# First-layer stream in threes of cycles, f16 parts of H on GpSimd, and both halves of V in one stationary operand, in a fused attention and feed-forward kernel

## The chip, the cores and the metric

One core of one Trainium2 chip runs the kernel. The metric is the device time in microseconds, the median of several runs. Engines are named as in the profile: PE (TensorE), ACT (ScalarE), DVE (VectorE), POOL (GpSimd), SP (SyncE).

## The reference

All inputs are float32; x is [1, 2048, 512], with 32 heads of 16 that share one K and one V, and a hidden layer of 1792.

```python
x = A_x
g = _sigmoid((x * gate_w).sum(-1, keepdims=True))
# attention, H = 32, Dh = 16
q = (x @ wq).reshape(B, S, H, Dh).transpose(0, 2, 1, 3)
k, v = x @ wk, x @ wv
p = softmax(einsum("bhqd,bkd->bhqk", q, k) * Dh ** -0.5)
a = einsum("bhqk,bkd->bhqd", p, v).transpose(0, 2, 1, 3).reshape(B, S, H * Dh) @ wo
# feed-forward
b = silu(x @ w1) @ w2
return g * a + (1 - g) * b
```

## The kernel before

float32 products are made from 16-bit parts: a number is split into an f16 part and an f16 remainder, and three products of parts stand for one product. A prologue (`first_pass`) transposes x, makes K and V and the first Q. Then `attention` runs one long stream.

The stream goes through 32 rounds: 4 blocks of 512 queries, 4 groups of 8 heads, and two halves of 4 heads each (`rb`). A round has 16 steps; a step is one tile of 128 keys. Two steps make a cycle, so there are 256 cycles, and one more that only drains. The order of PE's work in a cycle is written out by hand as a string of slots, each of eight matmuls on 64x32 tiles of the array with 512 columns:

- S: scores of one pair of heads-times-queries (`scores`), and behind it one exponential on ACT, 128x1024, into the tile P (float32). A cycle has four.
- F: eight matmuls of the other work (`stream`): Q blocks, the feed-forward's first layer (`ffn_h`, into H) and second layer (`ffn_o`), and the output projection (`out_proj`). An output (`Out`) has 12 products (6 in a group with two hidden tiles); the first half of the rows of a new output runs beside the second half of the one before.
- P: one third of the product of probabilities and V in 16-bit parts (`pv` with n = 0, 1, 2): the upper halves of P by VH, the same by VL, and the remainders L by VH. L is made on DVE by `low`, two instructions of 128x1024 for a step.
- N: the same product of a step straight in float32 (`pv` with n = 3, by VF).
- B: the bound of a Q block, where there is one.

The odd step of a cycle always goes through N. The even one goes through L and three P (SPLIT), or through N (NATIVE), as `split_step` decides when its L is to be made: not in a round's first step, and not when an output of the first layer is about to end. `debt` counts F slots that the Q blocks took beyond six a cycle; when it is 6 or more and a first-layer output has just ended, the next cycle is WIDE, with 12 F.

`spend` adds up DVE's work of a cycle in an account, `put` defers small DVE work by some cycles, and `fill` does deferred work, splitting of weights (`split_pieces`) and range checks (`chores`) while the account has room; what is over goes into `backlog`.

At the end of a first-layer output ACT makes e = tanh, DVE makes e = (e + 1) * ph, and later the two parts of H:

```python
H = Hs[k, f] = wp.tile([128, 2, 512], F16, name="H", bufs=2 * NF)
spend(0.62)
put(1.0, 2, lambda: split_v(H[:, 0], H[:, 1], e))
```

At the end of a round `norm_a` on DVE transposes the two PSUM banks of the product with V into T and U, adds them and divides by the row sums in column 16 (V carries a column of ones); `norm_b` and `norm_c` transpose back and split into f16 parts. The banks have one buffer. After the last cycle the remaining outputs run plainly (`whole`).

POOL has the start's memsets and issues the loads of raw weight tiles, each when DVE has used the tile before.

Of the kernel before, what the change touches and what calls it, by code (L numbers as in the profile page):

```python
# [6 lines left out]
F32 = mybir.dt.float32  # L7
# [16 lines left out]

SPLIT, NATIVE = "SFFFSFFFSPPPSBN", "SFFFSFFFSNBSN"
WIDE = {SPLIT: "SFFFFFFSFFFFFFSPPPBSN", NATIVE: "SFFFFFFSFFFFFFSNBSN"}
# [11 lines left out]
          (26, 27, 1.0, 6e4), (27, 28, 1.0, 6e4), (28, 29, 1.0, 6e4), (29, 30, 1.0, 6e4),  # L40
# [5 lines left out]
def kernel(  # L46
# [21 lines left out]
    nc = tc.nc  # L68
# [16 lines left out]
    VH = consts.tile([128, NKT, 32], F16)  # L85
    VL = consts.tile([128, NKT, 32], F16)
    VF = consts.tile([128, NKT, 32], F32)
    gg = consts.tile([128, NKT], F32)
# [119 lines left out]
    for t_ in (VH, VL, VF):  # L208
        nc.gpsimd.memset(t_, 0.0)
    nc.gpsimd.memset(VH[:, :, 16:17], 1.0)  # L210
    nc.gpsimd.memset(VF[:, :, 16:17], 1.0)
# [139 lines left out]
    def first_pass():  # L351
        with ExitStack() as pro:
# [132 lines left out]
            v_parts()  # L485
# [15 lines left out]
    def second_pass():  # L501
        with ExitStack() as pro:
# [81 lines left out]
            scales(sb, ps, ev, vm, (2.0 ** 13,))  # L584
            nc.vector.tensor_scalar(VF[:, :, 0:16], pv_[:, :, 0:16], ev[:, 0:1], None, op0=OP.mult)
            v_parts()
# [114 lines left out]
    def attention(ctx, scale_of, t_scale, shifts, split_pieces, chores, q_todo, bounds, early, gates_):  # L701
# [79 lines left out]
        def ffn_h(k, f):  # L781
            c, g = blocks[k]
            f0 = (sum(GF[:g]) + f) * 128
            cs = slice(c * 512, c * 512 + 512)

            def evict(ph):

                e = wp.tile([128, 512], F32, name="e", bufs=2)
                nc.scalar.activation(e, ph, AF.Tanh, scale=t_scale)  # L789
                nc.vector.scalar_tensor_tensor(e, e, 1.0, ph, op0=OP.add, op1=OP.mult)  # L790
# [69 lines left out]
        def outs():  # L860

            for k in range(len(blocks) + 1):
                if k < len(blocks):
                    for f in range(GF[blocks[k][1]]):
                        yield ffn_h(k, f)
                        while urgent:
                            yield urgent.pop(0)()
                else:
                    for _ in range(2):
                        yield urgent.pop(0)() if urgent else None  # L870
                if k:
                    for t in range(4):
                        if queue:
                            debt[0] += 12
                            yield q_block(queue.pop(0))
                        yield ffn_o(k - 1, t)
                        while urgent:
                            yield urgent.pop(0)()
            while True:
                yield urgent.pop(0)() if urgent else None  # L880
# [9 lines left out]
        seq, ahead, ended, debt = outs(), [], [None], [18]  # L890
        drains = [0]
# [4 lines left out]
        def stream():  # L896

            cur = None
            while True:
                if plain[0] and cur is None:  # L900
                    o = follow()
                    if o is None:
                        return
# [25 lines left out]
                cur = new  # L929
# [9 lines left out]
        def norm_a(pv, rb, st):  # L939
# [5 lines left out]
            nc.vector.tensor_tensor(T3[:, :, 0:17], T3[:, :, 0:17], U3[:, :, 0:17], op=OP.add)  # L945
# [80 lines left out]
        def pv(s, n):  # L1026
# [5 lines left out]
            if n == 3:  # L1032
                a, b = VF[:, k], probs.pop(s)
            else:
                while n == 2 and lq and lq[0][1] == s:
# [3 lines left out]
                if n == 2:  # L1039
                    probs.pop(s)  # L1040
# [22 lines left out]
        qtile, wide = {}, [False]  # L1063
# [3 lines left out]
        for s in range(0, len(steps) + 2, 2):  # L1067
# [7 lines left out]
            p, more = 2 * s, True  # L1075
            slots, order = SPLIT, [(s - 2, 0), (s - 2, 1), (s - 2, 2), (s - 1, 3)]
# [4 lines left out]
            wide[0] = debt[0] >= 6 and ended[0] is not None and ended[0].hidden  # L1081
            if wide[0]:
                slots = WIDE[slots]
            ended[0], n_f, bounded[0] = None, 0, False
            for a in slots:
# [5 lines left out]
                elif a == "F" and more:  # L1091
                    more = not next(work)
# [12 lines left out]
            fill(4.95 if n_f > 6 else 4.1 if ended[0] and ended[0].hidden else 3.7)  # L1105
# [39 lines left out]
```

## Time and profile before

| | |
|---|---|
| median of 3 runs | 1079.02 us (1078.17 to 1079.59) |
| span of the profiled execution | 1075.3 us; its own run time is not given |
| granted PE clock, mean | 0.998 |
| first exponential starts, last ends | 39.26 us, about 1054.2 us |
| PE, ACT, DVE, POOL busy | 1057.2, 1008.6, 789.9, 23.4 us |
| exponentials, tanh | 1024 and 56 |
| L instructions on DVE | 348, two for each of 174 split steps |

A row of a group reads: line, engine, operation, output<-inputs, shapes, count | busy us, mean ns of one | idle time of the engine ahead of it, and who ended it. A row of a timeline reads: start us, duration us, engine, line, operation, output<-inputs, count, and in brackets the idle time before. Successive matmuls overlap, so that the distance of two starts, not a duration, tells what a slot takes.

### The profile page before, as it was taken

What the parts mean: (1) busy time and instruction counts of PE and PEld (TensorE: products, weight loads), DVE (VectorE), ACT (ScalarE), POOL (GpSimd) and SP (SyncE); (2) the same over time, 40 slices, a digit from 0 to 9 for tenths busy, and PEclk for the clock granted to TensorE, in tenths of its full rate; (3) what the DMA queues carried; (4) which work ended last, traced back from release to release, by engine and by line L of the source; (5) the groups of instructions that cost most, each with busy time, mean ns of one, the idle gap of its engine ahead of it and who ended that gap; (6) DMA issues with size and microseconds to landing.
All of it is one profiled execution on the core that took longest, in us unless ns stands there. A gap on an engine that the chain in (4) does not pass through costs nothing.

```text
span 1075.3 us, 65967 instructions
## 1 busy us (share of the span) xinstructions
PE 1057.2 (98%) x31224; PEld 667.5 (62%) x31224; DVE 789.9 (73%) x1082; ACT 1008.6 (94%) x1121; POOL 23.4 (2%) x53
## 2 busy tenths in 40 slices
PE   8999999999999999999999999999999999999996
PEld 5455776766665577677655568677756555555552
DVE  6856986968778786878777697675857767476875
ACT  5799999999999999999999999899989999999992
POOL 2110000000000000000000000000000000000000
PEclk9999999999999999999999999999999999999999
DMA  5311111220001000000000100000000110000001
GB/s 208 115 61 45 49 42 31 61 60 14 11 11 41 32 22 10 17 12 12 22 11 21 37 19 21 22 12 11 20 6 12 31 31 12 11 11 5 11 4 43
DMA packets 20840, 32.95 MB, mean 31 GB/s; under 512 B 5137, under 2 KB 12050, under 8 KB 20562
## 3 DMA queue, kind: packets, MB, share of 16 engines
q1 hardware_dynamic: 17618, 20.46, 5.9%
q0 software_dynamic: 2512, 8.13, 2.6%
q8 instruction: 246, 4.03, 1.5%
q14 instruction: 32, 0.26, 0.1%
q10 hardware_dynamic: 432, 0.07, 0.0%
HBM read 20.12 MB, written 8.52 MB: 27 GB/s over the span
## 4 chain that ended last, share of the span: by engine, by line
PE 89%; DVE 5%; ACT 4%; issue 1%; POOL 0%; POOLq 0%; ACTq 0%
PE pv L1043 35%; PE pm L741 31%; PE S L997 19%; ACT P L1000 4%; DVE L L1021 1%; PE pm L745 1%; PE pt L311 0%; PE pk L126 0%; DVE xs L117 0%; DVE T L943 0%; PE pk L127 0%; PE pk L125 0%; DVE U L944 0%; PE pm L342 0%; DVE T L945 0%
## 5 line engine op out<-in xcount | busy, mean ns | idle before, releaser
L1000 ACT ACTIVATE P<-S 128x1024 f32<-128x1024 f32 x1024 | 963.5, 1051 | 24.6 <-PE S L997 19.4
L997 PE MATMUL S<-qb,KT 50*32 50x512 f16 x8192 | 480.1, 378 | 2.3 <-ACT P L1000 2.2
L1021 DVE TENSOR_TENSOR L<-P 128x1024 f16<-128x1024 f32 x348 | 408.1, 1217 | 8.3 <-ACT P L1000 8.2
L1043 PE MATMUL pv<-P,VF 64*32 64x512 f32 x5408 | 374.8, 589 | 0.0
L997 PEld LDWEIGHTS <-KT 50*32 50x32 f16 x8192 | 188.6, 90 | 193.9 <-issue 126.7
L741 PE MATMUL pm<-w2s,H 64*32 64x512 f16 x5232 | 258.8, 375 | 0.6 <-DVE qx L825 0.2
L741 PE MATMUL pm<-xs,w1s 64*32 64x512 f16 x5376 | 248.5, 375 | 1.1 <-issue 0.6
L741 PEld LDWEIGHTS <-H 64*32 64x32 f16 x5232 | 143.7, 93 | 43.5 <-issue 11.3
L741 PEld LDWEIGHTS <-w1s 64*32 64x32 f16 x5376 | 136.3, 93 | 46.1 <-issue 13.5
L1043 PEld LDWEIGHTS pv<-P,VF 64*32 64x32 f32 x5408 | 125.0, 107 | 30.3 <-issue 8.1
L790 DVE SCALAR_TENSOR_TENSOR e<-e,pm 128x512 f32<-128x512 f32 x56 | 38.5, 687 | 140.3 <-ACT e L789 139.4
L1043 PE MATMUL pv<-P,VH 64*32 64x512 bf16 x1392 | 81.9, 389 | 0.0
L1043 PE MATMUL pv<-L,VH 64*32 64x512 f16 x1392 | 81.4, 374 | 0.0
L1043 PE MATMUL pv<-P,VL 64*32 64x512 bf16 x1392 | 81.4, 385 | 0.0
L741 PE MATMUL pm<-xs,wqs 64*32 64x512 f16 x1152 | 81.1, 375 | 0.0
L1043 PEld LDWEIGHTS <-VH 64*32 64x32 f16 x2784 | 60.7, 92 | 20.4 <-issue 3.8
L741 PE MATMUL pm<-wo_s,O 64*32 64x512 f16 x1440 | 63.3, 375 | 0.0
L943 DVE STREAM_TRANSPOSE T<-pv 128x512 f32<-128x512 f32 x32 | 23.0, 717 | 48.0 <-PE pv L1043 40.4
L722 DVE SCALAR_TENSOR_TENSOR acc<-pm,g,acc 128x512 f32<-128x512 f32 x48 | 35.8, 745 | 26.4 <-PE pm L741 24.6
L741 PEld LDWEIGHTS <-wqs 64*32 64x32 f16 x1152 | 43.6, 93 | 10.1 <-issue 2.8
L121 DVE TENSOR_TENSOR H<-e,H 128x512 f16<-128x512 f32 x56 | 38.8, 693 | 1.9
L789 ACT ACTIVATE e<-pm 128x512 f32<-128x512 f32 x56 | 34.5, 616 | 5.7 <-PE pm L741 5.7
(155 smaller groups left out, 478.9 us busy)
## 6 DMA issues: line engine op xcount, KB each, us to landing
qb<-qd SPq DMA_DIRECT2D x192, 32.0 KB
raw<-in_B_w_dram POOLq DMA_DIRECT2D x23, 256.0 KB, 2.9
xn<-in_A_x_dram SPq DMA_DIRECT2D x8, 512.0 KB
out_dram<-acc SPq DMA_DIRECT2D x16, 256.0 KB
qd<-qx SPq DMA_DIRECT2D x12, 256.0 KB
raw<-in_A_wo_dram POOLq DMA_DIRECT2D x4, 256.0 KB, 3.6
qb<-sh SPq DMA_DIRECT2D x62, 2.0 KB
raw<-in_B_w_dram SPq DMA_DIRECT2D x3, 256.0 KB
```

The lines of the kernel that those rows point to most:

```text
L121: nc.vector.tensor_tensor(a2, a, a1, op=OP.subtract)
L722: nc.vector.scalar_tensor_tensor(a, po, gate[:, n:n + 1], a, op0=OP.mult, op1=OP.add)
L741: nc.tensor.matmul(self.bank[32 * m:32 * m + 32], l(i, rows, 32 * m), r(j, rows), start=first, stop=last)
L745: nc.tensor.matmul(self.bank, l(i, slice(0, 128), 0, 128), r(j, slice(0, 128)), start=first, stop=last)
L789: nc.scalar.activation(e, ph, AF.Tanh, scale=t_scale)
L790: nc.vector.scalar_tensor_tensor(e, e, 1.0, ph, op0=OP.add, op1=OP.mult)
L943: nc.vector.transpose(T, pv[0])
L997: nc.tensor.matmul(sc[32 * m:32 * m + 32, f], KT[b:b + 50, k0:k0 + 32], qtile[i][b:b + 50, j], start=True, stop=True)
L1000: nc.scalar.activation(P[:, 2 * j:2 * j + 2], sc, AF.Exp, scale=scale_of(c, o))
L1021: nc.vector.tensor_tensor(lows[s][:, q], P[:, q], upper(P)[:, q], op=OP.subtract)
L1043: nc.tensor.matmul(pvs[i][h][32 * j:32 * j + 32], a[r], b[r, j], start=first, stop=last)
```

## The change

Seven things change together.

1. V's halves go into one stationary operand VP of 32 columns: 16 upper columns, the ones, and 15 lower columns. The lower part of the column 0 is written as six digits into the rounding of the columns 1 to 6, which `v_parts` computes with some 25 more small DVE operations, and `norm_a` puts together again: it adds all 32 columns of T and U, multiplies six columns by the digits' weights, adds lower to upper columns, and sums the digits. A split step has two P slots in place of three.
2. `split_step` asks only for DVE's account: the step is split if `backlog` is below 1.0 (and it isn't the round's first).
3. WIDE is gone. When `debt` is 6 or more and a first-layer output with an even number has just begun, three cycles follow with 8 F slots each, the middle one with its P and N in another order.
4. The two parts of H are made on POOL, straight behind DVE's e.
5. Outputs of the output projection come in only after every second first-layer output.
6. The stream no longer ends early: the drain's F slots are kept, and `debt` starts at 0 where there are no Q blocks to come.
7. The range in which the maximum of V is accepted is narrower (512 to 8000), with another target scale in `second_pass`, which only runs when a range check fails.

In the built program 215 even steps are split and 41 are native. The cycles of the stream become 146 SPLIT, 28 NATIVE and 81 in threes (68 with two P, 13 native), besides the first and the drain.

```diff
-SPLIT, NATIVE = "SFFFSFFFSPPPSBN", "SFFFSFFFSNBSN"
-WIDE = {SPLIT: "SFFFFFFSFFFFFFSPPPBSN", NATIVE: "SFFFFFFSFFFFFFSNBSN"}
+SPLIT, NATIVE = "SFFFSFFFSPPSBN", "SFFFSFFFSNBSN"
+PAIR = ({SPLIT: "SFFFFSFFFFSPPSBN", NATIVE: "SFFFFSFFFFSNBSN"},
+        {SPLIT: "SFFFFSPPSNSFFFF", NATIVE: "SFFFFSNSNSFFFF"},
+        {SPLIT: "SFFFFSFFFFSPPSBN", NATIVE: "SFFFFSFFFFSNBSN"})
...
-    def v_parts():
-        nc.vector.tensor_copy(VH[:, :, 0:16], VF[:, :, 0:16])
-        nc.vector.tensor_tensor(VL[:, :, 0:16], VF[:, :, 0:16], VH[:, :, 0:16], op=OP.subtract)
+    def v_parts(pool):
+        n = 1 + DIGITS
+        R, r, J = (pool.tile([128, NKT, n], F32, name=f"v{q}") for q in "RrJ")
+        y = pool.tile([128, NKT, 1], F32, name="vy")
...
+        for d in range(1, n):
+            j = J[:, :, d:d + 1]
+            nc.vector.tensor_scalar(j, y, BASE, MAGIC, op0=OP.mult, op1=OP.add)
+            nc.vector.tensor_scalar(j, j, MAGIC, None, op0=OP.subtract)
+            if d < n - 1:
+                nc.vector.scalar_tensor_tensor(y, y, BASE, j, op0=OP.mult, op1=OP.subtract)
+        nc.vector.scalar_tensor_tensor(VP[:, :, 0:n], J, GRID, R, op0=OP.mult, op1=OP.add)
+        nc.vector.scalar_tensor_tensor(VP[:, :, 17:16 + n], J[:, :, 1:n], -GRID, r[:, :, 1:n], op0=OP.mult, op1=OP.add)
...
-                spend(0.62)
-                put(1.0, 2, lambda: split_v(H[:, 0], H[:, 1], e))
+                spend(0.69)
+                nc.gpsimd.tensor_copy(H[:, 0], e)
+                nc.gpsimd.tensor_tensor(H[:, 1], e, H[:, 0], op=OP.subtract)
...
-                         lambda j, b, kt=kt: xs[b, j, kt, cs]) for kt in range(KD)], evict, hidden=True)
+                         lambda j, b, kt=kt: xs[b, j, kt, cs]) for kt in range(KD)], evict, hidden=1 + f % 2)
...
-            nc.vector.tensor_tensor(T3[:, :, 0:17], T3[:, :, 0:17], U3[:, :, 0:17], op=OP.add)
+            nc.vector.tensor_tensor(T, T, U, op=OP.add)
+            z = U3[:, :, 0:DIGITS]
+            nc.vector.tensor_tensor(z, T3[:, :, 17:17 + DIGITS], mu[:, :, 1:].to_broadcast([128, 16, DIGITS]), op=OP.mult)
+            nc.vector.tensor_tensor(T3[:, :, 1:16], T3[:, :, 1:16], T3[:, :, 17:32], op=OP.add)
+            nc.vector.tensor_reduce(U3[:, :, 16:17], z, axis=AX.X, op=OP.add)
+            nc.vector.tensor_tensor(T3[:, :, 0:1], T3[:, :, 0:1], U3[:, :, 16:17], op=OP.add)
...
-            return steps[s][1] > 0 and not (turn[0] and turn[0].hidden and (0 < turn[1] <= 6 or wide[0]))
+            return steps[s][1] > 0 and backlog[0] < 1.0
...
-                a = (VH, VL, VH)[n][:, k]
-                b = lows.pop(s) if n == 2 else upper(probs[s])
+                a = VP[:, k]
+                b = lows.pop(s) if n else upper(probs[s])
...
-                spend(2.4)
+                spend(3.1)
...
-            wide[0] = debt[0] >= 6 and ended[0] is not None and ended[0].hidden
-            if wide[0]:
-                slots = WIDE[slots]
+            if not pair[0] and debt[0] >= 6 and s and turn[0] and turn[0].hidden == 1 and turn[1] == 12:
+                pair[0] = 3
+            if pair[0]:
+                slots = PAIR[3 - pair[0]][slots]
...
-            fill(4.95 if n_f > 6 else 4.1 if ended[0] and ended[0].hidden else 3.7)
+            fill(4.1 if pair[0] or ended[0] and ended[0].hidden else 3.7)
+            pair[0] = max(pair[0] - 1, 0)
```

More of the change, by code (lines that the diff above doesn't have):

```diff
@@ L865, in outs @@
                         yield ffn_h(k, f)
[L866 removed]
+                        while urgent and f % 2:
                             yield urgent.pop(0)()
@@ L888, in follow @@
             return o
-        seq, ahead, ended, debt = outs(), [], [None], [18]
-        drains = [0]
+        seq, ahead, ended, debt = outs(), [], [None], [18 if q_todo else 0]
+        drains, over = [0], [False]
         turn = [None, 0]
@@ L928, in stream @@
                     ended[0] = cur
-                cur = new
+                cur = turn[0] = new
+                turn[1] = 12
                 if cur:
@@ L1061, in early_products @@
                 yield
-        qtile, wide = {}, [False]
+        qtile, pair = {}, [0]
         whole_ = early_products()
@@ L1074, in attention @@
                     queue.append(q_todo.pop(0))
-            p, more = 2 * s, True
-            slots, order = SPLIT, [(s - 2, 0), (s - 2, 1), (s - 2, 2), (s - 1, 3)]
+            p = 2 * s
+            slots, order = SPLIT, [(s - 2, 0), (s - 2, 1), (s - 1, 3)]
             if s - 2 in native:
@@ L1090, in attention @@
                     next(whole_, None)
-                elif a == "F" and more:
-                    more = not next(work)
+                elif a == "F":
+                    next(work)
                     n_f += 1
```

41 lines of the change are left out of this document (28 added, 13 removed).

## The prediction

> **What bounds the kernel now.** I read the page first: busy shares, the chain that ended last, the costliest groups.
>
> ```profile
> span 1075.3 us, 65967 instructions
> PE 1057.2 (98%) x31224; PEld 667.5 (62%) x31224; DVE 789.9 (73%) x1082; ACT 1008.6 (94%) x1121; POOL 23.4 (2%) x53
> PE 89%; DVE 5%; ACT 4%; issue 1%; POOL 0%; POOLq 0%; ACTq 0%
> L1000 ACT ACTIVATE P<-S 128x1024 f32<-128x1024 f32 x1024 | 963.5, 1051 | 24.6 <-PE S L997 19.4
> L1021 DVE TENSOR_TENSOR L<-P 128x1024 f16<-128x1024 f32 x348 | 408.1, 1217 | 8.3 <-ACT P L1000 8.2
> ```
>
> PE carries the chain, but ACT is only a few per cent behind it. So the question is how much less PE work helps before ACT holds the end. The stream from the first exponential to the last, in the view by windows (busy PE, PEld, DVE, ACT, POOL), is
>
> ```profile
> 39.26:1054.20 1014.94, 1011.02 (x30944) 643.19 (x30946) 754.60 (x1001) 985.77 (x1080) 16.50 (x30) 1.00 0.08 24
> ```
>
> Two timelines give the prices inside it: first one whole SPLIT cycle on PE (lines of the F slots left out), then ACT.
>
> ```profile
> 598.20 0.41 PE L997 MATMUL S<-qb,KT 50*32 50x512 f16 x8
> 599.07 0.41 PE L997 MATMUL S<-qb,KT 50*32 50x512 f16 x8
> 599.94 0.41 PE L997 MATMUL S<-qb,KT 50*32 50x512 f16 x8
> 600.16 0.42 PE L1043 MATMUL pv<-P,VH 64*32 64x512 bf16 x8
> 600.38 0.42 PE L1043 MATMUL pv<-P,VL 64*32 64x512 bf16 x8
> 600.61 0.41 PE L1043 MATMUL pv<-L,VH 64*32 64x512 f16 x8
> 600.83 0.41 PE L997 MATMUL S<-qb,KT 50*32 50x512 f16 x8
> 601.04 1.05 PE L1043 MATMUL pv<-P,VF 64*32 64x512 f32 x16
> 601.90 0.41 PE L997 MATMUL S<-qb,KT 50*32 50x512 f16 x8
> ```
>
> ```profile
> 941.69 1.94 ACT L1000 ACTIVATE P<-S 128x1024 f32<-128x1024 f32 x2
> 943.51 0.60 ACT L789 ACTIVATE e<-pm 128x512 f32<-128x512 f32 x1
> 943.99 13.88 ACT L1000 ACTIVATE P<-S 128x1024 f32<-128x1024 f32 x15
> ```
>
> Not the durations count here (they overlap) but the starts. A slot of eight matmuls takes 0.22 us, whether S, F or P; the f32 slot N takes 0.86, that is four slots. The cycle has 4 S, 6 F, 3 P and one N: 17 slots in 601.90 - 598.20 = 3.70 us, **0.218 a slot**. ACT, when nothing holds it, starts an exponential every (943.51 - 941.69)/2 = **0.91 us** and loses **0.48** to a tanh. A cycle of four exponentials is 3.64, with a tanh 4.12.
>
> Before, by the order that the program is built in: 162 SPLIT cycles of 17 slots (3.70), 66 NATIVE of 18 (3.92; 35 of them with a tanh, 4.12), 11 and 16 wide ones of 23 and 24 slots (5.01, 5.23), and a first one of 5.0 (in both sums): 599.4 + 121.5 + 144.2 + 138.8 + 5.0 = 1008.9 us. The row says 1014.9, so 6 us are stalls. The wide cycles are PE's by far, 5.01 and 5.23 against ACT's 4.12.
>
> **The change, part by part.**
>
> *V joined and the split by account.* A split step costs PE two slots in place of three. In the built order 215 even steps are split (174 before) and 41 native. Together with the threes, the cycles become 146 SPLIT of 16 slots, 28 NATIVE of 18, and 81 in threes: 68 of 18 slots and 13 of 20. PE's share is then 16 x 0.218 = 3.49, below ACT's 3.64, in the 146: ACT sets them. The 28 stay at 3.92. A three with its two tanhs is ACT's too, 3 x 3.64 + 2 x 0.48 = 11.88 against PE's 54 x 0.218 = 11.77; a cycle of 20 slots adds 0.40.
> Sum: 146 x 3.64 + 28 x 3.92 + 27 x 11.88 + 13 x 0.40 + 5.0 + 1 (two tanhs elsewhere) = 531.4 + 109.8 + 320.8 + 5.2 + 6.0 = 973.2. **Less 35.7 us.** PE alone goes from 4583 to 4328 slots, 56 us less; the other 20 stay with ACT, whose floor lets a SPLIT cycle gain only 0.06, so nearly all of the gain is that of the wide and native cycles.
>
> *DVE's load.* It pays 82 more L at 1.14 (half of 2.27, the start-to-start pace of a pair) = 93 us, and a longer norm_a. It loses the H parts. Rows of both:
>
> ```profile
> L121 DVE TENSOR_TENSOR H<-e,H 128x512 f16<-128x512 f32 x56 | 38.8, 693 | 1.9
> L120 DVE CAST H<-e 128x512 f16<-128x512 f32 x56 | 23.7, 423 | 0.6
> L790 DVE SCALAR_TENSOR_TENSOR e<-e,pm 128x512 f32<-128x512 f32 x56 | 38.5, 687 | 140.3 <-ACT e L789 139.4
> L945 DVE TENSOR_TENSOR T<-T,U 128x272 f32<-128x272 f32 x32 | 14.2, 444 | 1.1
> L950 DVE TENSOR_TENSOR C<-T,rr 128x256 f32<-128x256 f32 x32 | 13.6, 425 | 1.1
> L947 DVE RECIPROCAL rr<-T 128x16 f32<-128x16 f32 x32 | 8.1, 254 | 1.1
> ```
>
> The parts go: 38.8 + 23.7 = 62.5 us. norm_a's addition grows from 0.44 to about 0.69 (the 128x512 row), and four operations are new: one of 240 elements (0.42), a product and a reduction of 96 (0.25 to 0.42 each), one of 16 (0.15 to 0.25): 1.4 us more a round. DVE comes to 754.6 + 93 - 62.5 + 31 x 1.4 = 829 us of about 979, 85% against 74%. It does not become the bound by sum; its lateness counts where PE needs an L.
>
> *At a round's end.* There norm_a stands ahead of the next L on DVE:
>
> ```profile
> 590.89 0.72 DVE L943 STREAM_TRANSPOSE T<-pv 128x512 f32<-128x512 f32 x1 [2.70 <-PE pv L1043]
> 593.35 0.74 DVE L722 SCALAR_TENSOR_TENSOR acc<-pm,gg,acc 128x512 f32<-128x512 f32 x1
> 594.01 4.62 DVE L1021 TENSOR_TENSOR L<-P 128x1024 f16<-128x1024 f32 x4
> ...
> 596.90 0.41 PE L1043 MATMUL pv<-L,VH 64*32 64x512 f16 x8
> ```
>
> The first pair of L is done at 594.01 + 2.27 = 596.28, and PE asks for it at 596.90. With 1.4 more it is done at 597.68; PE asks one slot earlier, about 596.67, and waits 1.0. Behind that P stands the next S, and behind it ACT. But where ACT is the bound PE is 0.91 - 0.22 = 0.69 ahead of it, so 0.3 is lost: 31 x 0.3 = **9 us**. Ends: 0 where no operation of another part stands between, 31 x 1.4 = 43 with no lead at all.
>
> *H parts on POOL.* Before, POOL does almost nothing:
>
> ```profile
> L178 POOL DMA_DIRECT2D raw<-in_B_w_dram x27 | 14.7, 544 | 186.0 <-DVE w1s L196 99.8 <-DVE w2s L196 64.0 <-DVE wqs L196 14.2
> L304 POOL COPY wkv<-wvr 128x64 f32<-128x64 f32 x1 | 0.2, 237 | 0.0
> L305 POOL COPY wkv<-gwr 128x4 f32<-128x4 f32 x1 | 0.2, 190 | 1.0 <-DMA gwr<-in_gate_w_dram 1.0
> ```
>
> The two copies differ by 47 ns for 60 elements, so a copy of 512 is some 0.19 + 0.40 = 0.59 us; the subtraction, with two operands, from the same to 0.19 + 2 x 0.40 = 0.99. That is 1.2 to 1.6 us for an H, 56 x 1.6 = 90 us of an idle engine. H is read a block later, so nobody waits for it, and the tile e has two buffers against an H every 1.5 cycles. Behind each part on POOL stand the raw weight loads (27 of w1 and w2 by the row, six others): a load now waits up to a tanh and two parts more, some 4 us, and its raw tile is asked for three cycles (11 us) later. I cost that at nothing; with that cover gone it would be 4 us for each of the loads that come late, which ends with the last weight.
> Whether POOL slows DVE no row of before shows, for POOL computes nothing while DVE does. Ends: a gain of 0 (DVE isn't the bound) and all of POOL's time taken from DVE. A three gives DVE 6 L (6.8), two e (1.4) and 3/8 of a norm_a of 3.9 (1.4), 9.6 of 11.88: 2.2 us are free, 1.1 for each H. As 1.2 to 1.6 is near that, I take 0.1 for each of 54: **5 us**.
> [...]
>
> *The start.* v_parts grows by 25 operations: 18 on 128x16 (0.17 each by the row below), seven on 112 elements a partition (0.2 to 0.25): 3.1 + 1.6 = 4.7 us more on DVE.
>
> ```profile
> L329 DVE TENSOR_SCALAR gg<-gg 128x16 f32<-128x16 f32 x1 | 0.2, 169 | 0.0
> ```
>
> ```profile
> 39.76 0.69 DVE L824 TENSOR_SCALAR O<-pm 128x512 f16<-128x512 f32 x1 [1.72 <-PE pm L745]
> 40.49 0.69 DVE L825 SCALAR_TENSOR_TENSOR O<-pm,O 128x512 f16<-128x512 f32 x1
> 42.50 0.39 PE L342 MATMUL pm<-qx,kab 64*32 64x512 f16 x2
> ```
>
> DVE has 1.72 idle ahead of the first eviction, and the matmul that takes over the evicted bank comes 42.50 - 41.18 = 1.3 after it. 4.7 - 1.7 - 1.3 = 1.7, rounded to **2 us**. Ends: 0 and 4.7.
>
> *The end.* The last norm_a is on the path (1.4), and 24 plain products stand there for 18:
>
> ```profile
> 1060.41 4.47 PE L745 MATMUL pm<-wo_s,O 128*128 128x512 f16 x12 [2.21 <-DVE O L120]
> 1064.90 4.04 PE L745 MATMUL pm<-w2s,H 128*128 128x512 f16 x18
> ```
>
> 6 x 4.04/18 = 1.3, together **3 us**.
>
> Sum: 1075.3 - 35.7 + 9 + 5 + 2 + 3 = 1058.6, the 6 us of stalls left in. No time of the profiled execution itself is given; the median of the runs, 1079.02, lies 3.7 above its span. **Forecast 1062 us.**
>
> **The rivals.**
>
> *ACT runs free.* The lead of 0.69 hides norm_a and POOL, and most of the old 6 us too: 1062 - 9 - 5 - 5 = 1043. For it: what ACT waited for ahead of an exponential was PE, 19.4 of 24.6 us, and PE now has slots to spare. Against: the L of the round's end above stood only 0.62 ahead of PE, before DVE's load grew.
>
> *DVE late at more places.* At every round's end 0.7 instead of 0.3, by the same row with an eviction more: 12 us more, 1074.
>
> *POOL holds DVE (slower than before).* Beside an L each part takes DVE's turn. If all 1.6 of an H are lost to DVE, 0.5 beyond the free 1.1, it costs 54 x 0.5 = 27 instead of 5: 1084. The point from which it decides: slower than 1081 from 0.45 beyond the free time, 1.55 us an H. For it: L follows e directly on DVE, just when POOL begins. Against: a part that comes first delays one L, and DVE is idle behind many an e (the 139.4 us of its row).
> [...]
>
> *The change doesn't do what it says.* That fewer steps are split than meant, or that cycles stay wide, the built order excludes.
>
> **How the numbers follow.** Forecast 0.56 (its own range 1050 to 1070); ACT free 0.18 (1040 to 1050); DVE late 0.15 (1070 to 1080, a fifth of it within 0.2% of before, about what a measurement here can tell from no change); POOL holds DVE 0.11. Faster 0.86, same 0.03, slower 0.11. 1041 to 1078 leaves out about 0.16.
>
> **What would show it.** Right: P slots go in pairs, SPLIT cycles at 3.6 to 3.7 with exponentials at 0.91 without idle, threes near 11.9, ACT's busy share at 96% or more, PE's idle rows before P named after DVE's L and only behind norm_a. Wrong: threes over 12.3 with L lasting longer than 1.22 or starting late beside POOL (the last rival), or a SPLIT cycle below 3.6 (then ACT's floor is lower than 0.91). If the first exponential starts 4 us later, v_parts was mis-costed.

## The result, and the profile after

The changed kernel is slower: 1094.35 us (median of 4 runs, 1092.31 to 1097.11) against 1079.3 us for the kernel before in the same session (4 runs, 1078.17 to 1080.89). The ratio is 1.0144, with a 95% interval of 1.0125 to 1.0163. The forecast was 1062 us and its range ended at 1078, so direction and size were both wrong.

The page of the kernel after, in the rows that answer to those of before: span, busy shares, the chain that ended last, the exponentials, L.

```profile
span 1095.2 us, 63374 instructions
PE 1050.2 (96%) x29790; PEld 577.0 (53%) x29790; DVE 899.7 (82%) x1206; ACT 1012.1 (92%) x1121; POOL 215.0 (20%) x170
PE 66%; DVE 26%; ACT 5%; issue 2%; DMA 0%; another core or an unknown queue 0%; ACTq 0%; POOL 0%; DVEq 0%
L1035 ACT ACTIVATE P<-S 128x1024 f32<-128x1024 f32 x1024 | 968.4, 1067 | 44.0 <-PE S L1032 32.8
L1056 DVE TENSOR_TENSOR L<-P 128x1024 f16<-128x1024 f32 x430 | 531.0, 1281 | 11.1 <-ACT P L1035 11.1
```

And the stream, from the first exponential to the last, in the view by windows (busy PE, PEld, DVE, ACT, POOL):

```profile
39.38:1071.20 1031.82, 1001.38 (x29468) 551.41 (x29474) 860.76 (x1109) 989.03 (x1080) 208.82 (x142) 1.00 0.09 24
```

What to see: in the chain DVE went from 5% to 26%, and PE from 89% to 66%. The exponentials wait longer for PE's scores (32.8 us, 19.4 before), although PE issues 1434 fewer matmuls. In the stream DVE was to be busy 829 us of 979; it is busy 861 of 1032, 83%. PE is busy 97% of it, ACT 96% and DVE 83%, and in the chain they take turns: they wait for each other. The window ends 0.2 us before the last exponential, at 1071.38; with that the stream grew by 17.1 us (1014.9 to 1032.0) and what comes behind it by 2.7.

The cycles by kind, from the start of every fourth exponential in the trace (sums over the kind, us):

| kind | count | forecast | after | after, DVE's extra work gone (after_all_short) |
|---|---|---|---|---|
| SPLIT | 146 | 531.4 | 551.0 (median 3.64, mean 3.77) | 539.8 |
| NATIVE | 28 | 109.8 | 121.4 | 113.5 |
| in threes | 81 | 326.0 | 351.8 | 344.5, a pause of about 5 in it |
| first | 1 | 5.0 | 7.6 | 5.0 |

Half of the SPLIT cycles do run at the forecast pace; the mean is what the forecast missed. The last column is a run of experiment 9 below, which leaves work out. Three places in the trace show why.

**A round's end.** Timelines of DVE, PE and ACT in the kernel after, around the end of a round that falls into the middle of a three (some DVE lines left out):

```profile
504.20 0.72 DVE L973 STREAM_TRANSPOSE T<-pv 128x512 f32<-128x512 f32 x1 [2.85 <-PE pv L1078]
...
507.89 0.71 DVE L989 STREAM_TRANSPOSE T<-C 128x512 f32<-128x512 f32 x1
508.53 0.65 DVE L815 SCALAR_TENSOR_TENSOR e<-e,pm 128x512 f32<-128x512 f32 x1
509.10 2.76 DVE L1056 TENSOR_TENSOR L<-P 128x1024 f16<-128x1024 f32 x2
511.78 1.39 DVE L124 CAST O<-T 128x512 f16<-128x512 f32 x1
```

```profile
507.53 0.42 PE L1032 MATMUL S<-qb,KT 50*32 50x512 f16 x7
509.23 0.37 PE L766 MATMUL pm<-xs,wqs 64*32 64x512 f16 x1 [1.28 <-DVE e L815]
```

```profile
505.43 0.62 ACT L814 ACTIVATE e<-pm 128x512 f32<-128x512 f32 x1
505.90 3.11 ACT L1035 ACTIVATE P<-S 128x1024 f32<-128x1024 f32 x3
510.63 2.05 ACT L1035 ACTIVATE P<-S 128x1024 f32<-128x1024 f32 x2 [1.62 <-PE S L1032]
```

The tanh is done at 506.05, but e, which empties its PSUM bank, starts only at 508.53: in DVE's queue it stands behind the whole of norm_a (504.20 to 507.85) and norm_b's transpose, which follows at once (to 508.60). PE's next F slot needs that bank, waits, and the score behind it and the exponential behind that wait too, 1.62 us on ACT. It isn't the L that is late, as I had it, but the eviction. That cycle takes 6.1 us; five of the six native middle cycles do.

**The start.** PE's timeline, DVE's, and the window of the first two cycles:

```profile
42.39 0.41 PE L1032 MATMUL S<-qb,KT 50*32 50x512 f16 x8
44.86 0.39 PE L367 MATMUL pm<-qx,kab 64*32 64x512 f16 x2 [2.06 <-DVE O L851]
```

```profile
35.95 0.23 DVE L343 CAST VP<-VF 128x144 f16<-128x144 f32 x1
...
42.05 0.25 DVE L359 SCALAR_TENSOR_TENSOR VP<-vJ,vr 128x96 f16<-128x96 f32 x1
...
44.11 0.69 DVE L851 SCALAR_TENSOR_TENSOR O<-pm,O 128x512 f16<-128x512 f32 x1
```

```profile
39.40:58.00 18.60, 16.54 (x248) 7.30 (x254) 14.95 (x38) 12.04 (x13) 2.51 (x4) 0.82 0.38 112
```

v_parts holds DVE from 35.95 to 42.30. The first exponential isn't later (39.38 against 39.26), but the eviction behind v_parts is, PE stands 2.06 us, and then the granted clock halves: 0.82 in the window, which is half speed for 6.8 of 18.6 us. The first two cycles take 7.58 and 6.95 us, 5.01 and 3.95 in the kernel before.

**DVE's and POOL's new groups.** Rows of the groups, kernel after:

```profile
L818 POOL CAST H<-e 128x512 f16<-128x512 f32 x56 | 85.2, 1521 | 641.3 <-DVE e L815 639.9 <-issue 1.5
L819 POOL TENSOR_TENSOR H<-e,H 128x512 f16<-128x512 f32 x56 | 106.5, 1902 | 4.5
L975 DVE TENSOR_TENSOR T<-T,U 128x512 f32<-128x512 f32 x32 | 22.4, 700 | 1.1
L977 DVE TENSOR_TENSOR U<-T,mu 128x96 f32<-128x96 f32 x32 | 8.3, 259 | 1.1
L978 DVE TENSOR_TENSOR T<-T 128x240 f32<-128x240 f32 x32 | 12.8, 401 | 0.0
L979 DVE TENSOR_REDUCE U<-U 128x16 f32<-128x96 f32 x32 | 7.9, 246 | 0.0
L980 DVE TENSOR_TENSOR T<-T,U 128x16 f32<-128x16 f32 x32 | 6.1, 191 | 1.1
```

norm_a grew by (0.700 - 0.444) + 0.259 + 0.401 + 0.246 + 0.191 = 1.35 us a round: sized right, placed wrong. An H costs POOL 3.42 us where I had 1.2 to 1.6, and an L 1281 ns in place of 1217.

### The profile page after: what moved, and what is told of

It is laid out like the page before. It is cut to its first block, busy times and chain, and to the rows that moved or that the text cites. A ratio compares the mean times of both kernels' runs of the same rounds, so it can differ in the third digit from the quotient of the medians.

```text
span 1095.2 us, 63374 instructions
## 1 busy us (share of the span) xinstructions
PE 1050.2 (96%) x29790; PEld 577.0 (53%) x29790; DVE 899.7 (82%) x1206; ACT 1012.1 (92%) x1121; POOL 215.0 (20%) x170
## 4 chain that ended last, share of the span: by engine, by line
PE 66%; DVE 26%; ACT 5%; issue 2%; DMA 0%; another core or an unknown queue 0%; ACTq 0%; POOL 0%; DVEq 0%
PE pv L1078 23%; PE pm L766 23%; PE S L1032 16%; DVE L L1056 10%; ACT P L1035 4%; DVE T L975 1%; DVE T L973 1%; DVE U L974 1%; DVE e L815 1%; ACT e L814 1%; PE pm L770 1%; DVE O L124 1%; DVE mxs L139 1%; DVE C L985 1%; DVE acc L747 1%
## 5 line engine op out<-in xcount | busy, mean ns | idle before, releaser
L1035 ACT ACTIVATE P<-S 128x1024 f32<-128x1024 f32 x1024 | 968.4, 1067 | 44.0 <-PE S L1032 32.8
L1056 DVE TENSOR_TENSOR L<-P 128x1024 f16<-128x1024 f32 x430 | 531.0, 1281 | 11.1 <-ACT P L1035 11.1
L1078 PE MATMUL pv<-P,VF 64*32 64x512 f32 x4752 | 333.1, 593 | 0.0
L818 POOL CAST H<-e 128x512 f16<-128x512 f32 x56 | 85.2, 1521 | 641.3 <-DVE e L815 639.9
L766 PEld LDWEIGHTS <-w1s 64*32 64x32 f16 x5376 | 119.2, 93 | 64.3 <-issue 20.9
L766 PEld LDWEIGHTS <-H 64*32 64x32 f16 x5184 | 120.4, 93 | 60.4 <-issue 18.8
L1078 PEld LDWEIGHTS pv<-P,VF 64*32 64x32 f32 x4752 | 103.0, 107 | 29.4 <-issue 4.0
L1078 PE MATMUL pv<-L,VP 64*32 64x512 f16 x1720 | 113.6, 375 | 4.5 <-DVE L L1056 3.4
L819 POOL TENSOR_TENSOR H<-e,H 128x512 f16<-128x512 f32 x56 | 106.5, 1902 | 4.5
L1078 PEld LDWEIGHTS <-VP 64*32 64x32 f16 x3440 | 71.0, 93 | 54.0 <-issue 29.4
L1078 PE MATMUL pv<-P,VP 64*32 64x512 bf16 x1720 | 99.4, 388 | 0.0
```

Source lines behind the costliest of these rows:

```text
L766: nc.tensor.matmul(self.bank[32 * m:32 * m + 32], l(i, rows, 32 * m), r(j, rows), start=first, stop=last)
L818: nc.gpsimd.tensor_copy(H[:, 0], e)
L819: nc.gpsimd.tensor_tensor(H[:, 1], e, H[:, 0], op=OP.subtract)
L1035: nc.scalar.activation(P[:, 2 * j:2 * j + 2], sc, AF.Exp, scale=scale_of(c, o))
L1056: nc.vector.tensor_tensor(lows[s][:, q], P[:, q], upper(P)[:, q], op=OP.subtract)
L1078: nc.tensor.matmul(pvs[i][h][32 * j:32 * j + 32], a[r], b[r, j], start=first, stop=last)
```

## The experiments

Ratios are to the kernel before, run beside each (its medians all lay near 1079 us); the kernel after stands at 1.0144. Differences between kernels are taken between ratios, 0.001 being 1.08 us.

**1. H parts back on DVE, where POOL made them.** Is it POOL that slows DVE down?

```diff
-                nc.gpsimd.tensor_copy(H[:, 0], e)
-                nc.gpsimd.tensor_tensor(H[:, 1], e, H[:, 0], op=OP.subtract)
+                split_v(H[:, 0], H[:, 1], e)
```

> The changed kernel with the two parts of H on DVE, at the same place and with the same account, so that the order of PE's work stays. If POOL's parts hold DVE's two-operand instructions (3.4 us of POOL for each H in the changed kernel's trace), this is faster than 1094 by 10 to 25 us, though DVE has 1.1 us more of its own for each H, and L falls back from 1281 to about 1217 ns. If the longer norm_a ahead of the evictions is what costs, it is no faster than 1094, rather 5 to 15 us slower, as DVE has 62 us more to do.

1111.38 us, ratio 1.0297 [1.028, 1.0314]: 16.5 us slower than after, a little more than the 5 to 15 expected if norm_a is what costs. Its L and its PE wait, from the groups and the waits (us, times, longest); the like wait in after is 3.4 us:

```profile
L1055 DVE TENSOR_TENSOR L<-P 128x1024 f16<-128x1024 f32 x430 | 503.0, 1217 | 8.6 <-ACT P L1034 8.6
```

```profile
PE pv L1077 <- DVE L L1055: 18.1, 32, 1.0
```

L alone is 1217 again, so POOL does lengthen it; but 1.1 us of parts ahead of L cost far more than that. In this kernel the move to POOL helps, so the rival on the slower side does not explain the loss; what POOL's reads cost by themselves experiment 5 shows.

**2. The kernel before with the H parts on POOL.**

```diff
-                put(1.0, 2, lambda: split_v(H[:, 0], H[:, 1], e))
+                put(1.0, 2, lambda: None)
+                nc.gpsimd.tensor_copy(H[:, 0], e)
+                nc.gpsimd.tensor_tensor(H[:, 1], e, H[:, 0], op=OP.subtract)
```

> The kernel before with the parts of H on POOL and nothing else changed. If POOL holds DVE, L and CAST grow where they meet a part, and the time is 1079 to 1090 although DVE loses 62 us of work. If POOL costs DVE nothing, it is 1076 to 1079, since in the old kernel PE is the bound.

1079.67 us, ratio 1.0006 [0.9996, 1.0016]: no change. L is lengthened here nearly as much, and nothing comes of it where DVE has room and gives up 62 us of parts:

```profile
L1023 DVE TENSOR_TENSOR L<-P 128x1024 f16<-128x1024 f32 x348 | 427.2, 1273 | 10.5 <-ACT P L1002 10.4
```

**3. norm_a without the digits' four operations** (the lower columns are left out).

```diff
-            nc.vector.tensor_tensor(T, T, U, op=OP.add)
...
-            nc.vector.tensor_tensor(T3[:, :, 0:1], T3[:, :, 0:1], U3[:, :, 16:17], op=OP.add)
+            nc.vector.tensor_tensor(T3[:, :, 0:17], T3[:, :, 0:17], U3[:, :, 0:17], op=OP.add)
```

> The changed kernel with norm_a as short as before (the lower columns and the digits are left out of the sum, so only upper halves come out). If the longer norm_a ahead of evictions and L is what costs, the cycles of 6 us at the round's ends fall below 5 and the time goes to 1065 to 1080. If POOL's parts are the cost, it stays within 5 us of 1094.

1076.35 us, ratio 0.9973 [0.9963, 0.9982]: 18.5 us of the kernel after go with 32 x 1.35 = 43 us of DVE work. The 6.1 us cycles become 4.99, the native ones of 5.98 become 4.86, SPLIT's sum falls from 551.0 to 543.2. The first F slot behind such a norm_a on PE:

```profile
498.87 0.37 PE L766 MATMUL pm<-xs,wqs 64*32 64x512 f16 x1 [0.16 <-DVE e L815]
```

0.16 us in place of 1.28. PE's waits for e, by the waits view of after and of this run:

```profile
PE pm L766 <- DVE e L815: 7.1, 6, 1.3
PE pm L766 <- DVE e L815: 0.8, 5, 0.2
```

With the waits for the other evictions (qx, acc) PE stands 20.2 us of the stream, from 58 us on, in after and 6.3 here; these 14 us less of waiting are most of the 18.5. Eight of the SPLIT cycles that fall, from 4.25 to 3.63, are a round's second cycle and wait for such an eviction too. Of the costs taken out one by one this is the largest.

**4. V's parts by two operations** (the lower part of column 0 is left out).

```diff
-        n = 1 + DIGITS
...
+        nc.vector.tensor_copy(VP[:, :, 0:16], VF[:, :, 0:16])
+        nc.vector.tensor_tensor(VP[:, :, 17:32], VF[:, :, 1:16], VP[:, :, 1:16], op=OP.subtract)
```

> The changed kernel with V's parts made by two operations (no digits; the lower part of V's column 0 is left out). If the start costs what the trace shows (the first two cycles 14.5 us against 8.8, part of it at half of PE's clock), the time is 1094 - 5.7 = 1088 to 1089. If the half clock has another cause than PE's wait for DVE, only some 2 us go: 1092.

1090.09 us, ratio 1.0103 [1.0086, 1.012]: 4.4 us. The first cycle is 5.01 again and no half clock follows it: the next 13 exponentials run in 12.87 us without idle. Up to 5.7 were expected with the half clock and 2 without it; how much of a run is at half clock differs between runs of one kernel (last section).

**5. POOL writes constants into H and reads nothing.**

```diff
-                nc.gpsimd.tensor_copy(H[:, 0], e)
-                nc.gpsimd.tensor_tensor(H[:, 1], e, H[:, 0], op=OP.subtract)
+                nc.gpsimd.memset(H[:, 0], 0.01)
+                nc.gpsimd.memset(H[:, 1], 0.0)
```

> The changed kernel with POOL writing constants into both parts of H instead of computing them (the parts are left out, POOL reads nothing); all else and the order of work as in the changed kernel. If the two engines meet where both read, L falls from 1281 to about 1217 ns and CAST O from 723 to 421, 430 x 64 ns = 28 us of DVE go, and the time falls from 1094 by 5 to 15 us. If the lengthened L do not reach the end, it stays within 3 us of 1094.

1091.24 us, ratio 1.0117 [1.01, 1.0134]: 2.9 us, less than the 5 to 15 expected. L is back at its old length, 1217 ns on average over all 430, though POOL still writes both parts of H (0.53 us each), so what lengthens L comes with the parts that read. (The casts of O on DVE are not back at 421 ns but at 544, from 723.) L's row:

```profile
L1056 DVE TENSOR_TENSOR L<-P 128x1024 f16<-128x1024 f32 x430 | 503.0, 1217 | 9.0 <-ACT P L1035 9.0
```

**6 and 7. The same work later.** First norm_a's transposes at once and the rest at the end of the next cycle; then v_parts too, moved behind the first cycle's work.

```diff
+            def rest():
...
+            due.append((cycle[0] + 1, rest))
...
-                spend(3.1)
+                spend(1.4)
...
+            while due and due[0][0] <= cycle[0]:
+                due.pop(0)[1]()
             fill(4.1 if pair[0] or ended[0] and ended[0].hidden else 3.7)
```

> The changed kernel with norm_a cut in two: the two transposes at once, which free the banks, and the rest at the end of the cycle after. All work is kept; the account moves with it, so that some steps change between split and native. If PE's F slots wait for evictions that stand behind norm_a, the cycles of 6.1 us at the round's ends fall to about 4.3 and the time to 1075 to 1084. If it is the amount of DVE work that counts and not its place, it stays at 1090 to 1096.

1085.58 us, ratio 1.0056 [1.0035, 1.0077]: 9.5 us, half of what leaving the work out gave. With the account some cycles change their kind; those that took 6.1 us now take 3.95 to 4.34. But now the L behind the moved rest is late (waits view; 3.4 us in after):

```profile
PE pv L1087 <- DVE L L1065: 13.4, 21, 0.9
```

```diff
-            v_parts(sb)
             note()
...
+            if s == 0 and shifts == 1:
+                v_parts(wp)
+                spend(4.7)
```

> norm_a cut in two as in the other run and, besides, V's digits made at the end of the first cycle instead of ahead of it. If the two costs are separate, 4 to 6 us less than norm_a cut alone: 1070 to 1079. If the first cycles then wait for V's parts instead, no less.

1083.33 us, ratio 1.0034 [1.0021, 1.0047]; 2.4 us more, where 4 to 6 were expected; the first cycle takes 5.01. Moving the work to a later place is not enough here; experiment 10 moves it to another engine.

**8. Joined V alone, in the order of before** (wide cycles, the old rule of splitting, H parts on DVE).

```diff
-SPLIT, NATIVE = "SFFFSFFFSPPPSBN", "SFFFSFFFSNBSN"
-WIDE = {SPLIT: "SFFFFFFSFFFFFFSPPPBSN", NATIVE: "SFFFFFFSFFFFFFSNBSN"}
+SPLIT, NATIVE = "SFFFSFFFSPPSBN", "SFFFSFFFSNBSN"
+WIDE = {SPLIT: "SFFFFFFSFFFFFFSPPBSN", NATIVE: "SFFFFFFSFFFFFFSNBSN"}
```

> The kernel before with V's halves joined (two P slots, long norm_a, digits) and nothing else: wide cycles, the old rule for splitting, H's parts on DVE. By the kinds of cycles 162 x 0.06 = 10 us less, less 11 x 0.2 = 2, plus 6 for the start and up to 18 for norm_a: 1079 to 1091. If norm_a's length costs only where a first-layer output ends at a round's end, which the wide cycles also meet, it is 1073 to 1079.

1089.22 us, ratio 1.0081 [1.0054, 1.0107]: slower than before. SPLIT cycles have a median of 3.64 and a mean of 3.745, against a mean of 3.736 before, so inside the stream what the dropped slot gives is lost again; that norm_a takes it is likely but not separated here. The trace is 11.9 us longer than that of before: 5.6 of these are the first two cycles (7.72 and 6.80), 2 the end, and about 5 a pause near 803 us (see Open below).

**9. Experiments 3, 4 and 5 at once** (what they leave out is left out here too).

```diff
+            nc.vector.tensor_tensor(T3[:, :, 0:17], T3[:, :, 0:17], U3[:, :, 0:17], op=OP.add)
...
+        nc.vector.tensor_copy(VP[:, :, 0:16], VF[:, :, 0:16])
...
+                nc.gpsimd.memset(H[:, 0], 0.01)
```

> The changed kernel without the three added costs at once: short norm_a, V's parts by two operations, POOL writing constants into H (lower columns, digits and the parts of H are left out). If the three costs add up, 1094 - 18 - 4 - 3 = 1069. If they hide one another, down to 1050, near the forecast's sum without them (1046). What is left above 1046 then belongs to the order of slots itself: threes at 12.3 instead of 11.9 make 11 of it.

1065.39 us, ratio 0.9873 [0.9854, 0.9893]: 29.2 us under after; the three alone give 18.5 + 4.4 + 2.9 = 25.8. This is about what the new order of slots is worth when DVE pays nothing for it. Against the forecast without its three costs of that kind, 1062 - 9 - 2 - 5 = 1046, 19 us are still missing. The last column of the table has them: the threes 13.4 (344.5 less the pause of about 5, less 326.0), the pause itself, SPLIT 8.4 and NATIVE 3.7, together 30.6. Of these 6 were in the sum as old stalls and 1 as the two tanhs elsewhere. Against the 23.6 that are left, the end is 2.7 us shorter than forecast, and the time lies 1.6 above the span where 3.7 was taken.

**10. norm_a's additions and product on POOL, the small rest on DVE a cycle later; v_parts late.** All the work is done.

```diff
-            nc.vector.tensor_tensor(T, T, U, op=OP.add)
+            nc.gpsimd.tensor_tensor(T, T, U, op=OP.add)
...
-            nc.vector.tensor_tensor(T3[:, :, 1:16], T3[:, :, 1:16], T3[:, :, 17:32], op=OP.add)
+            nc.gpsimd.tensor_tensor(T3[:, :, 1:16], T3[:, :, 1:16], T3[:, :, 17:32], op=OP.add)
```

> All work kept: norm_a's transposes at once on DVE, its additions and the product on POOL, the reduction, reciprocal and product at the end of the cycle after; V's digits at the end of the first cycle. If DVE's amount of work ahead of L and of evictions is the cause, DVE has 1.3 us less a round than in the changed kernel and none of it in front of an eviction: 1066 to 1076, faster than before. If POOL's parts beside L take as much from DVE as they give, 1080 to 1085 as with both late.

1072.04 us, ratio 0.9938 [0.9921, 0.9954]: faster than before, by 0.6%. Busy shares (page), POOL's first addition (groups) and PE's wait for L (waits):

```profile
PE 1038.7 (97%) x29790; PEld 577.3 (54%) x29790; DVE 872.2 (82%) x1102; ACT 1010.4 (94%) x1121; POOL 324.4 (30%) x266
```

```profile
L976 POOL TENSOR_TENSOR T<-T,U 128x512 f32<-128x512 f32 x32 | 50.3, 1573 | 369.7 <-DVE U L975 369.7
```

```profile
PE pv L1086 <- DVE L L1064: 3.2, 8, 0.7
```

The same addition that takes DVE 0.70 us takes POOL 1.57, and POOL has the time. The kernel is 22 us faster than after: 12 of these experiment 7 already had by the later place, and 10 come with POOL (1.0034 to 0.9938). (DVE's account changes with it, 211 even steps are split in place of 215, and 210 in experiment 7. The trace has no pause of over 1 us near 790, which may be some of the 10.)

**11. The third cycle of a three in the middle one's order**, on 10.

```diff
-        {SPLIT: "SFFFFSFFFFSPPSBN", NATIVE: "SFFFFSFFFFSNBSN"})
+        {SPLIT: "SFFFFSPPSNSFFFF", NATIVE: "SFFFFSNSNSFFFF"})
```

> The same, and the third cycle of a three in the middle one's order (P and N ahead of the last eight F slots), so that no tanh waits in the middle of a cycle for PE. If ACT's wait for the tanh's input is what makes a three 12.3 instead of 11.9, the threes fall to 12.1 and the time by 4 to 8 us against the same kernel without it. If PE's slots set the threes, no change, or slower by some us since L is asked for earlier.

1101.59 us, ratio 1.0205 [1.0186, 1.0224]; a miss. The third cycle stays at 4.25 (the middle one takes 4.09), and the cycle behind the three now waits (waits view: 1.4 us in 10; then one place on PE):

```profile
PE pm L765 <- DVE e L814: 38.2, 26, 2.1
```

```profile
440.57 1.06 PE L765 MATMUL pm<-xs,w1s 64*32 64x512 f16 x32 [1.27 <-DVE e L814]
```

This order ends an output with the cycle's last slot; its tanh then stands behind the exponentials on ACT, while PE's next F slots want the bank. The bank is what is short again.

**12. Experiment 8 with the late v_parts and norm_a on POOL.**

```diff
-            v_parts(sb)
             note()
...
+            if s == 0 and shifts == 1:
+                v_parts(wp)
...
-            nc.vector.tensor_tensor(T, T, U, op=OP.add)
+            nc.gpsimd.tensor_tensor(T, T, U, op=OP.add)
```

> The kernel before with joined V alone, with V's digits after the first cycle and norm_a's additions on POOL, the rest of it late; wide cycles, old rule, parts of H on DVE. If the joined V was only spoiled by its start and its longer norm_a, 1066 to 1073. If PE's saved slots bring nothing while wide and native cycles stay, 1074 to 1079.

1087.19 us, ratio 1.0076 [1.0058, 1.0093]; another miss: the old rule splits step 2, whose P then waits for the late v_parts,

```profile
52.66 0.58 PE L1078 MATMUL pv<-P,VP 64*32 64x512 bf16 x8 [2.66 <-DVE VP L356]
```

and that cycle takes 10.7 us, some 7 too many. Without these the kernel would stand near 1080, and without the pause of nearly 6 us that this trace has near 790, near 1074. Whether the joined V gains something in the old order this run doesn't settle.

**13 and 14. The tanh of a third cycle held back until behind the next score**, on 9 and on 10. A clean three takes 4.05 + 4.09 + 4.245 us. Does the third lose its 0.13 above 4.12 because ACT waits at the tanh for its input?

```diff
-                    cur.evict(cur.bank)
+                    if pair[0] == 1 and cur.hidden and not plain[0]:
+                        held.append(cur)
+                    else:
+                        cur.evict(cur.bank)
```

> The changed kernel without its three added costs (as in the run that leaves out all three: lower columns, digits and the parts of H), and in the third cycle of a three the tanh and what follows it stand one exponential later on ACT and DVE. If ACT's wait for the tanh's input is why a clean three takes 12.3 us instead of 11.9, the third cycles fall from 4.24 to about 4.1 and the time from 1065 by 3 to 6 us. If PE's eighteen slots set the three, it stays at 1065.

> The correct kernel at 1072 (norm_a's additions on POOL, the rest late, digits late), with the tanh of the third cycle one exponential later. By ACT's wait alone 3 to 6 us less, 1066 to 1069; L of that cycle then also stands ahead of the e that waits for the tanh, which can give 2 to 4 more. If PE sets the three, 1071 to 1073.

1078.18 us, ratio 0.9988 [0.9978, 0.9998], and 1080.82 us, ratio 1.0018 [1.0009, 1.0027]: 12 and 9 us slower than their bases. The third cycle goes to 4.48. ACT had no idle ahead of the tanh to begin with, so that theory falls. The waits view shows where the later tanh costs: its e is late too, and PE's F slots want the bank (0.8 us, 5 times, in experiment 9; this is its late variant):

```profile
PE pm L747 <- DVE e L796: 18.1, 32, 0.8
```

On 10 the same wait goes from 1.4 to 17.7 us. The starts of the exponentials show the rest. In a split third cycle of experiment 9 their distances have medians of 1.04, 1.40 (with the tanh), 0.90 and 0.90; with the late tanh they are 1.04, 1.14, 1.40 and 0.90. So the 0.13 is the first distance, where ACT waits for the five slots of PE (1.08, less a small lead) and does not go at its own 0.91, and a tanh that moves on to the next distance no longer covers the five slots of the one it left.

**15 and 16. The same slots at other distances**, on 10. In the first cycle of a split three the distances between two S are, in slots, 5, 5, 3, 5. If only the cycle's sum counts, moving an F changes nothing. If PE can run ahead of ACT by no more than one exponential (S has two PSUM buffers), each distance counts by itself.

```diff
-PAIR = ({SPLIT: "SFFFFSFFFFSPPSBN", NATIVE: "SFFFFSFFFFSNBSN"},
+PAIR = ({SPLIT: "SFFFFSFFFSPPFSBN", NATIVE: "SFFFFSFFFFSNBSN"},
```

That is the even one (5, 4, 4, 5); the uneven one (7, 3, 3, 5) has

```diff
+PAIR = ({SPLIT: "SFFFFFFSFFSPPSBN", NATIVE: "SFFFFSFFFFSNBSN"},
```

> The correct kernel at 1072 with one F slot of the first cycle of each three moved behind its two P slots, so that its S slots stand 5, 4, 4, 5 slots apart instead of 5, 5, 3, 5. If only the number of slots in a cycle counts, 1072 as before. If each distance between two S counts by itself against ACT's 0.91 (S has two buffers, so PE cannot save time for a later distance), 0.1 to 0.2 less in each first cycle: 1067 to 1070.

> The same kernel with the S slots of each three's first cycle 7, 3, 3, 5 apart, the same eighteen slots. If only their number counts, 1072. If each distance counts, 0.3 to 0.45 more in each first split cycle: 1078 to 1083.

Even: **1070.44 us**, ratio 0.9916 [0.9903, 0.993], the fastest here that does all the work, ahead of before by 0.8% and just above the 1067 to 1070 expected. Uneven: 1075.62 us, ratio 0.9961 [0.9948, 0.9975]. The two, run side by side, differ clearly; against 10 each interval still overlaps, and the cycles carry the argument. The medians of that cycle are 3.86 even, 3.99 as it was, 4.18 uneven, with 18 slots (3.92) in each. Scores on PE in one such cycle of the uneven kernel:

```profile
533.84 0.41 PE L1040 MATMUL S<-qb,KT 50*32 50x512 f16 x8
535.35 0.41 PE L1040 MATMUL S<-qb,KT 50*32 50x512 f16 x8
536.00 0.41 PE L1040 MATMUL S<-qb,KT 50*32 50x512 f16 x8
536.91 0.41 PE L1040 MATMUL S<-qb,KT 50*32 50x512 f16 x8
537.98 0.41 PE L1040 MATMUL S<-qb,KT 50*32 50x512 f16 x8
```

Seven slots take 1.51, ACT's 0.91 has run dry; the next three take 0.65, PE's pace; the next three 0.91, ACT's pace, because PE may not run further ahead; then five, 1.07. The sum is 4.14 and not 3.92, the pace of 18 slots without a wait; if every distance counted by itself it would be about 4.4 (1.53 + 0.91 + 0.91 + 1.09). So neither rule holds in full: the distances count, but a lead of one exponential does carry over from one to the next. That is why the uneven kernel lost less than the 0.3 to 0.45 a cycle that were expected, and stayed below 1078.

## Why the prediction was wrong

It was wrong in two steps above all: what a round's end costs, 9 us taken and 18.5 measured, and how a three is summed, 11.88 us taken and 12.39 found.

*Right.* ACT's floor: SPLIT cycles have a median of 3.64, the middle cycle of a three 4.09 (4.12 forecast). The counts of cycles. norm_a's growth, 1.35 for 1.4. What comes behind the stream, 2.7 for 3. That POOL lengthens L, and that it is worth little: I took 5 us, it measures 2.9.

*A round's end, 9 us taken, 18.5 measured.* I priced the one wait that the quoted rows showed, L's behind norm_a, at 0.3 us a round. That wait, PE's for L, is 3.4 us in the whole of after. What norm_a also holds up is every eviction in DVE's queue, 20.2 us of waits on PE. PE's F slots have two PSUM banks; where an output ends beside a round, the bank comes free only behind norm_a, and PE, then ACT, stand 1 to 2 us. My upper end of 43 held it, the value I took did not. I should have asked for everything behind the longer list in that queue, not only for what waited in the profile of before.

*The threes, 11.88 us forecast, 12.39 clean.* I set ACT's sum of a three against PE's, 11.88 against 11.77, and took the larger. But PE can bank one exponential at most (experiment 16: three slots in 0.65, the next three in 0.91). The first cycle has 18 slots and no tanh and is PE's (3.92 by the slots, mostly 3.8 to 4.06 in the traces, by the lead it starts with), the others are mainly ACT's, and the maxima add; in the third one PE's first distance adds 0.13. Together that is 27 x 0.5 = 13.4 us. Experiments 13 to 16 show the mechanism.

*SPLIT cycles, 3.64 forecast, 3.77 on average: 20 us.* The step "DVE does not become the bound by sum" was right and didn't settle anything. At 83% busy, with all of its work in one queue, DVE is at places late by more than the 0.15 us that PE has over in such a cycle (3.64 less 3.49), and what goes beyond is lost to ACT. With the extra work gone the SPLIT sum falls by 11 of these 20, 8 of them with norm_a's part alone (experiment 3), so this is largely the round's end once more; of the rest the kernel before has its share, as its SPLIT cycles too had a mean 0.03 above their median of 3.71.

*The start, 2 us taken, 4.4 measured.* The stall itself was seen at the right place; that half clock could follow it was not in the sum.

*POOL.* The forecast's copy, 0.59 us, was right for POOL by itself (0.61); the subtraction was put at 0.99 at most and takes 1.17. Nearly half of an H's 3.42 us is what the two take beyond 0.61 and 1.17, beside DVE's work (below). The rival on the slower side had a mechanism that is there but far too small, and the right sign by chance: an H lengthens L by 0.49 us on DVE, well under the 1.1 that I had put as free, and taking that away gives 2.9 us. Its sign, threes over 12.3 with an L longer than 1.22, did come true, but it could not tell this rival from the other causes. "DVE late at more places" was nearest: it put 12 us on the forecast, to 1074, where 32 were missing, because it took one eviction more at a round's end, and no other place.

Sum: 1046 (forecast without DVE's and POOL's costs) + 19 (threes, SPLIT, NATIVE and the pause, experiment 9) = 1065; + 18.5 + 4.4 + 2.9 = 1091, and 3 us more where they meet: 1094.

*Open.* Many of the traces have a pause of 1.5 to 6 us between 760 and 805 us, for which the profile names no cause. It is about 1.5 us in before, about 3.8 in after (with 3.4 us of half clock behind it) and 5 in experiments 3 and 9; experiments 10, 15 and 16 show none over 1 us. So at most 2.3 of the 15 us between before and after can be its, but that is as much as some differences between the experiments. Each kernel has one trace here, so whether it changes from one run to the next stays open.

## What to carry to other kernels

With three engines above 80%, price a cut on one of them by the pair that is next, distance by distance between the slots that hand work over; a sum over a cycle is only as good as the buffers that carry a lead across it. When work is added to an in-order queue, list everything behind it that frees a buffer, evictions first: 43 us of off-path DVE work cost 18.5 us here, most of them as waits of PE for PSUM banks. An engine with 70% idle is the place for such work even where it takes twice as long: doing norm_a's rest and v_parts later and the additions on POOL, at 1.57 us for 0.70, turned 1.4% slower into 0.6% faster, about half of it by POOL, and with even distances into 0.8%.

## What the runs showed of the hardware

**POOL and DVE lengthen each other's operations.** One H of the kernel after beside a pair of L, DVE's timeline and POOL's:

```profile
300.79 2.77 DVE L1056 TENSOR_TENSOR L<-P 128x1024 f16<-128x1024 f32 x2
300.94 1.54 POOL L818 CAST H<-e 128x512 f16<-128x512 f32 x1 [1.06 <-DVE e L815]
302.56 2.03 POOL L819 TENSOR_TENSOR H<-e,H 128x512 f16<-128x512 f32 x1
```

And one of experiment 10, with transposes and a reduction on DVE but no L:

```profile
489.56 0.61 POOL L817 CAST H<-e 128x512 f16<-128x512 f32 x1 [22.69 <-DVE e L814]
490.25 1.17 POOL L818 TENSOR_TENSOR H<-e,H 128x512 f16<-128x512 f32 x1
```

POOL's two operations take 0.61 and 1.17 us alone, 1.54 and 2.03 beside L: 0.9 us more each. The pair of L takes 2.77, where a pair without POOL's parts beside it takes 2.35. The durations come in such steps and hardly between them: in the trace of after L takes 1.18 to 1.23 us 372 times, 1.53 to 1.63 fifty times and 2.18 eight times; POOL's subtraction takes 1.15 to 1.17 eight times and 2.01 to 2.03 forty-eight times. With POOL only writing (experiment 5) L is back at 1217. The trace also shows who pays: POOL loses 1.6 us of an H on average (3.42 less 1.78) and L on DVE 0.49 (430 x 64 ns over 56), and POOL's loss is free, for in the waits of after no engine waits for an H. The subtraction takes DVE 0.69 us (the kernel before) and POOL 1.17 alone, 1.7 times as long, and 1.90 on average here, 2.7 times.

**Half clock behind stalls of 2 us.** In the kernel after, a stall of PE of 2.06 us at the start was followed by half clock from 46.0 to 52.8 us, and one of 2.04 us, to 1078.49, by half clock from 1080.2 to 1083.6. Five stalls of 1.57 to 1.65 us in the same trace have none behind them. In experiment 12, behind a stall of 2.66 us, two S with an N between them start 2.11 us apart (55.88 and 57.99), where it was 1.08 ahead of the stall (46.61 and 47.69). The price is not fixed: the four runs of after have mean granted clocks from 0.993 to 0.997, by which some 15 us of one and 7 us of another were at half clock (an estimate: twice the share missing from 1, times the span). The length of one stall alone doesn't decide either: half clock from 793.5 to 796.9 in after stands behind the pause named above, in which no idle of PE is longer than 0.67 us.
